# One of three bit shifts of VectorE's exponentials done by accumulating DMAs, with a ring of four PSUM banks, exponentials of two tiles and 133 packs on VectorE

## The chip, the core and the metric

The kernel runs on one core of a Trainium2 chip. The core has TensorE (PE, matmuls; its weight loads are shown as PEld), VectorE (DVE), ScalarE (ACT), GpSimd (POOL) and SyncE (SP), each with a queue of its own that it works through in order, and 16 DMA engines that all queues share. On-chip memory is SBUF (128 partitions) and PSUM (8 banks of 128 x 512 fp32, where matmuls write). The metric is device microseconds of one execution; the median of some runs is compared.

## The reference

Two attention blocks over the same x (2048 tokens, 512 features, 32 heads of 16) are mixed by a gate. Block A is softmax attention over all 2048 x 2048 pairs of each head, which is nearly all of the work. Block B is linear attention with softmax features.

```python
g = sigmoid((x * gate_w).sum(-1, keepdims=True))
# A: scores = q @ k.T * 16**-0.5 ; p = softmax(scores) ; o = p @ v ; a = o @ A_wo
# B: phi = [softmax(q @ w_phi), softmax(-(q @ w_phi))], the same for k
#    kv = phi_k.T @ v ; z = phi_k.sum ; b = (phi_q @ kv / (phi_q @ z + 1e-6)) @ B_wo
out = g * a + (1 - g) * b
```

## The kernel before

**Block A by packs.** A unit is one head's scores of 128 keys against 512 queries, one PSUM bank. Four units (four heads, whose 16 features sit in four 32-row strips of TensorE, so their score matmuls run side by side) make a pack; 16 packs (`kt`, the key tiles) make a group, and 32 groups (four query chunks of eight) make the 512 packs. A pack's probabilities, 128 keys x 512 queries for each head, are multiplied with V by four matmuls in four 32-column strips, which add up over a group's 16 packs in one PSUM bank. V carries a column of ones, so the same matmuls give the softmax denominator.

**Two ways to an exponential.** Most packs go over ACT: `_qk` (matmuls of L963) writes scores into a ring of `RING = 5` banks, `_exp` (L1011) turns three and two tiles in turn into bf16 in the buffer ET, `_pv` (L1077) multiplies with V. The score matmuls of one exponential wait for the exponential two before it, which read the same banks; in PE's queue they come first when they can run. The other packs, listed by `AWAY` (five bits for each group, for the tiles `KT0 + KTS * n`, here 1, 4, 7, 10, 13), go over VectorE: 121 packs. `_vector_bits` (L903) computes one tile as `uint16(score * a + b)`, whose bits, read as bf16, are a piecewise linear exponential. To smooth it, the sum of four such numbers is used, whose bits are shifted by 0, 30, 62 and 95; the last two are multiplied with a copy `vc` of V scaled by 0.75. `_vector_terms` (L919) makes the three shifted copies in the buffer `vp` from the buffer `va`, for two packs (4096 elements a partition) or one (2048) at a time, and `_pv_terms` multiplies each of the four with V on PE, again L1077. So a VectorE pack costs DVE four tiles of L903 and three shares of L919, and PE sixteen matmuls where an ACT pack needs four. `va` holds two pairs of packs.

**Banks.** The banks outside the ring are shared: one holds the group's sum, one or more are lent to each projection, VectorE score tile or output in turn (`acquire`, `release`).

**The order of the work** is set in Python before anything runs. Each instruction is an `Op` with engine, assumed cost, dependencies and a priority `prio` counted in packs; `Plan.order` puts the ops of each engine into a fixed order by these costs, and `SHIFT` moves the priorities of some hundred ops by hand-given amounts. `LAT`, `TURN`, `lat=` are assumed latencies. `emit` writes the queues with semaphore waits. So a wait on the chip that is longer than was assumed is not reordered: the queue stands. `_fill` (L1084) and the loop in `_qk` (L984) put filler matmuls where PE would have little to do.

**Around it.** `_proj_*` compute K, Q, V and evict them with DVE (L656, L664, L675, L697, L720); Q goes on by DMA from SP (L677). `_norm` divides a group's sum by its denominators on DVE and sends it by DMA (L1148) and a transposing DMA (L1363) to the output projection (L1457); the last group is normalized by `_norm_last` in two halves without DMA (L1107 to L1117). `_gate` computes the gate for the four query chunks by four matmul groups on TensorE (L736) and four transposes (L741). Block B's softmaxes run on DVE and ACT between (L1252 to L1309; the ACT part is L1281).

Of the kernel before, what the change touches and what calls it, by code (L numbers as in the profile page):

```python
# [22 lines left out]
SHIFTS = ((30, 0), (62, 1), (95, 1))  # L23
# [20 lines left out]
class Op:  # L44
    def __init__(self, eng, fn, cost, name, prio, rel, kind, lat):
        self.eng, self.fn, self.cost, self.name = eng, fn, cost, name
        self.prio, self.rel, self.kind, self.lat = prio, rel, kind, lat
        self.deps = []
        self.users = []
        self.left = 0  # L50
        self.need = False
        self.acquire = None
        self.release = None
        self.sem = None
        self.start = self.end = None
        self.commit = None
        self.array = 0.0
        self.filler = 0
        self.slack = None
        self.fits = True  # L60
        self.pad = False
        self.tiles = []
        self.filled = 0
        self.tag = None

# [38 lines left out]
class Plan:  # L104
# [190 lines left out]
    def emit(self, nc, ctx):  # L295
# [6 lines left out]
        count = dict.fromkeys(self.ENGS, 0)  # L302
        for e, q in self.queues.items():
            for o in q:
                if o.name.startswith("dma"):
# [71 lines left out]
class _Kernel:  # L377
    RING = 5
# [4 lines left out]
    NB, LEAD = 4, 16.0  # L383
    FIRST = 5
    KT0, KTS, NKT = 1, 3, 5
    KEEP = 13
    GAP, KDUE, VDUE, GATE = 3.45, -16.25, -11.75, 14.0
    TURN = 1.5
    LAST, RAMP, PART = 8.0, 48, 24
    STEP, BITS, TERM, PVX, NORM, QDUE, PUT = 0.625, -80, 5.5, 0.8, 2, -22.0, 3.8  # L390
# [29 lines left out]
    def _memory(self, ctx):  # L420
# [54 lines left out]
        self.va = sb("va", [P, 2, 2, self.NB, QCH], U16)  # L475
        self.warm = self.bq[:, 0, 0:QCH]
        self.wpp = self.bq[:, 3, 0:4 * P].rearrange("p (c j) -> p c j", c=4)
        self.gwb = self.bq[:, 0, QCH:2 * QCH].rearrange("p (c m) -> p c m", c=4)
# [59 lines left out]
    def _consts(self):  # L538
# [21 lines left out]
        self.b_zero, self.b_warm, self.b_gwb = B(), B(), B()  # L560
        op("DVE", lambda e: e.memset(self.warm, 1.0), 0.3, writes=[self.b_warm], prio=-95)
# [24 lines left out]
    def _projections(self):  # L586
# [13 lines left out]
        for j in range(NQC):  # L600
            if j == 0:
# [3 lines left out]
                self._proj_k0(1, 4)  # L605
# [61 lines left out]
    def _proj_q(self, qc, cp):  # L667
# [12 lines left out]
                 prio=due, lat=1.6)  # L680
# [44 lines left out]
    def _gate(self):  # L725
        op, NQC = self.plan.op, self.NQC
        b_gwb, last = self.b_gwb, []
        op("POOL", lambda e: e.tensor_copy(self.gwb, self.gw[:, :, None].to_broadcast([P, 4, P])), 1.0,
           reads=[self.b_gw], writes=[b_gwb], name="gwb", prio=15)
        z = self.onTA[:].rearrange("p s r j -> p (s r j)").bitcast(F32).rearrange("p (q b d) -> p q b d", q=NQC, d=32)  # L730
        for qc in range(NQC):
            job = Job()

            def mm(e, qc=qc, job=job):
                for c in range(4):
                    ins = e.matmul(self._bank(job), self.gwb[:, c, :], self.xT[:, c, QCH * qc:QCH * qc + QCH],  # L736
                                   start=(c == 0), stop=(c == 3))
                return ins
            m = op("PE", mm, 4 * self.c_pe(512), reads=[self.b_xT[qc], b_gwb], name="gate", prio=self.GATE + qc, rel=self.GATE - 6,
                   acquire=job)  # L740
            last.append(op("DVE", lambda e, qc=qc, job=job: e.transpose(  # L741
                z[:, qc].rearrange("p b d -> p (b d)"), self._bank(job)), 0.74, deps=[m], name="gate_t", prio=self.GATE + qc,
                release=job))
        flat = self.gh[:].rearrange("p r q b -> p (r q b)")
        col = z[:, :, :, 0].rearrange("p q b -> p (q b)")
        for r, sign in ((0, -1.0), (1, 1.0)):
            last.append(op("DVE", lambda e, r=r, sign=sign: e.tensor_scalar(
                self.gh[:, r].rearrange("p q b -> p (q b)"), col, sign, None, op0=ALU.mult), 0.2,
                deps=last, name="gate_z", prio=22))
        for b in self.b_onTA[0] + self.b_onTA[1]:  # L750
            b.readers = last[-2:]
        a = op("ACT", lambda e: e.activation(flat, flat, ACT.Exp), 0.2, deps=last, name="gate_exp", prio=24)
        self.b_g = Buf()
        op("DVE", lambda e: e.tensor_scalar(flat, flat, 1.0, None, op0=ALU.add), 0.25, deps=[a], writes=[self.b_g],
           name="gate_h", prio=24)
# [9 lines left out]
    AWAY = (15, 3, 9, 7, 27, 30, 29, 28, 26, 14, 15, 31, 14, 15, 27, 15, 15, 31, 23, 22, 31, 27, 13, 30, 27, 23, 11, 29, 31, 31, 21, 31)  # L765

    SHIFT = (
        ("p12", 11.5), ("k5", 3.5), ("k4", -8.5), ("v1", -2.5), ("p30", 10.5), ("p6", 13), ("p13", 1), ("p22", 7),
        ("p15", -5), ("q1", 3), ("w0", -13.5), ("p18", 6), ("b1", -9.5), ("v2", -4.5), ("x1", 2), ("v4", 6), ("p21",
        8), ("p2", 1), ("k1", -3), ("p26", -1.5), ("k6", 2), ("b4", -2.5), ("p9", -2), ("p0", 4.5), ("b42", 0.5),  # L770
        ("x4", -7.5), ("b20", -4), ("b55", 2.5), ("p40", 4), ("b52", -6.5), ("g1", 10), ("p36", 2), ("p38", 7),
        ("x33", -0.5), ("p31", 8), ("d0", -3.5), ("p34", -0.5), ("p32", -6.5), ("p39", 1), ("v9", 7), ("b68", -8.5),
        ("b65", -10.5), ("e2", -3.5), ("p62", -8), ("p54", -2), ("p47", -4), ("p59", -0.5), ("x77", 6), ("b87", 4),
        ("x65", 5.5), ("t84", -7.5), ("t65", 0.5), ("p75", -3), ("p70", 0.5), ("x68", -6), ("p72", 4.5), ("b93",
        6.5), ("x55", 11), ("b77", 5.5), ("b90", 7.5), ("a0", -1.5), ("p89", 1), ("p79", -0.5), ("g4", 9), ("x90",
        10), ("b97", 11.5), ("p92", 5), ("p94", 6.5), ("p104", 10.5), ("e5", -1.5), ("g5", 1.5), ("x103", -3),
        ("t90", 12), ("p98", -7.5), ("e4", -6), ("g6", 12), ("q5", 1.5), ("p124", -6), ("x138", -4), ("x122", 5),
        ("p140", -1.5), ("p126", -10.5), ("g7", 2), ("p127", -10), ("p121", 6.5), ("x141", -12), ("p116", -0.5),
        ("p137", -13.5), ("t125", -9), ("p113", -2), ("b132", -2.5), ("b125", -8.5), ("b138", -8), ("a4", -9),
        ("p136", -12), ("x109", 11), ("b154", 8.5), ("e8", 6), ("p112", 5.5), ("g8", 1), ("p152", 11), ("e11",  # L780
        -10.5), ("p157", -3), ("p149", -13.5), ("p158", -8), ("t154", -5), ("b170", 6), ("p155", 8.5), ("t148", 1),
        ("e9", 6), ("p147", -0.5), ("p144", 2.5), ("b167", 3), ("p171", 2.5), ("p172", 10), ("p159", 8), ("p168",
        8.5), ("p163", -7.5), ("p162", 0.5), ("a8", 9), ("x177", 11.5), ("p192", -11.5), ("p194", 2.5), ("p188",
        -2), ("g11", 1.5), ("e13", -1.5), ("p190", -8), ("x199", 10.5), ("p181", 8), ("b199", -4.5), ("p184", 11.5),
        ("p195", -2.5), ("b196", -5.5), ("d12", -13.5), ("p219", 4), ("x209", -13), ("p207", -8), ("p210", -8),
        ("p204", -8.5), ("t209", 11), ("p203", 3), ("p232", 12.5), ("p233", 8), ("f0", -5.5), ("b241", 8.5),
        ("x234", 3.5), ("t225", 12), ("a12", 14), ("p254", 3.5), ("p240", -14), ("b260", -1), ("p245", -11.5),
        ("p242", -13), ("b234", -12.5), ("p236", -8), ("b263", -11), ("g14", 2), ("p251", 12.5), ("b257", 8), ("h0",
        -8), ("t257", -11), ("t241", 2), ("b279", -3), ("x260", 13.5), ("p256", 3.5), ("p255", 8), ("p268", 6),
        ("p246", -0.5), ("p264", 2), ("p270", -3.5), ("p258", -1.5), ("p274", 5), ("p284", 2), ("g16", -11.5),  # L790
        ("x257", 6), ("b301", -8.5), ("p277", 9.5), ("p286", 3), ("p275", -11.5), ("p272", -2), ("t279", 10),
        ("b289", 7.5), ("b285", -0.5), ("p287", 14), ("p291", -5.5), ("b311", 3), ("p307", 2.5), ("p296", 1.5),
        ("p303", 2), ("p294", -4), ("b324", -10.5), ("p315", 8), ("p306", -12), ("t289", -5.5), ("x311", 8),
        ("p300", 10.5), ("p302", 14), ("x289", -4), ("o0", -8), ("p304", 8), ("x292", 8), ("p297", 5), ("p293", 2),
        ("b327", -6), ("h5", -10.5), ("n5", -9), ("x317", -3), ("o3", 3), ("p318", -4), ("n4", -9), ("p332", -4),
        ("p323", 2), ("p331", 4.5), ("q11", 0.5), ("b333", 13.5), ("p338", -9.5), ("p341", -1), ("x349", 14),
        ("h10", -7), ("p380", -10), ("p371", 6.5), ("p363", 6.5), ("p376", 12.5), ("o4", -8), ("o5", -3), ("p377",
        -1), ("b372", -13.5), ("h8", -4.5), ("x372", 8.5), ("o6", -11.5), ("h9", 10.5), ("p367", -0.5), ("p374",
        -1), ("p373", 2), ("x359", -9), ("g21", -1.5), ("p366", -6), ("x381", -4), ("b381", 1.5), ("x362", -2.5),
        ("p386", -1), ("p396", 0.5), ("b397", 5.5), ("n9", -4.5), ("b417", 13.5), ("f3", -8), ("b413", 2), ("b404",  # L800
        6), ("p414", -1.5), ("x385", 0.5), ("p411", -2), ("p409", 1.5), ("p392", 3.5), ("p400", 8), ("p416", -5.5),
# [717 lines left out]
```

## Time and profile before

| | |
|---|---|
| median of 3 runs | 759.11 us (758.89 to 759.82) |
| the profiled execution | 759.64 us, its span 757.8 us |
| granted TensorE clock | 0.999 |
| ACT busy | 740.4 us, of it L1011 712.2 |
| DVE busy | 730.0 us, of it L903 314.4 and L919 221.6 |
| PE busy | 718.0 us |
| POOL busy | 8.1 us, all in the first 60 us |
| DMA | 21.68 MB, at most 78 GB/s in a slice after the first two |

The span runs from the first to the last instruction; the execution's own time is a little longer. Busy time is the union of an engine's records: two instructions of one engine can overlap in the records, so the mean length of one is longer than the step from one to the next. The idle time "before" a group says what the engine waited for; a wait of an engine that is not the bound costs nothing. In the chain of work in order of time, each piece is either work or an engine's queue, and its length is what it adds to the end.

### The profile page before, as it was taken

To read this page: it belongs to the slowest core of one execution; us is meant where nothing else is said; L and a number is where in the kernel's file an instruction comes from. 1 tells how busy PE (TensorE), PEld (TensorE's weight loads), DVE (VectorE), ACT (ScalarE), POOL (GpSimd) and SP (SyncE) were. 2 spreads that over 40 slices of the span, in tenths; PEclk is the share of its full clock that TensorE was granted. 3 is DMA by queue.
4 is the path that set the end of the run, shared out by engine and by line. 5 is a ranking of instruction groups with operands and counts; after the bars stand their busy time and mean duration, and the time that the engine had idled before them with its cause. 6 is when DMAs were issued, how large, how long until landed. Compare 5 with 4: busy or idle time off the path is not lost.

```text
span 757.8 us, 16775 instructions
## 1 busy us (share of the span) xinstructions
PE 718.0 (95%) x7172; PEld 229.8 (30%) x7241; DVE 730.0 (96%) x1138; ACT 740.4 (98%) x646; POOL 8.1 (1%) x17
## 2 busy tenths in 40 slices
PE   8999999999999999999999999999999998999997
PEld 3334333342322232232222222223232222222222
DVE  6989899999999999999999999999999999999997
ACT  6999999999999999999999999999999999999995
POOL 3000000000000000000000000000000000000000
PEclk9999999999999999999999999999999999999999
DMA  9300100000010010000003101411103102301120
GB/s 212 130 2 1 15 8 10 14 7 16 2 16 8 8 16 8 6 11 7 18 9 63 23 12 25 71 29 23 29 29 65 21 16 35 78 13 25 12 26 29
DMA packets 88745, 21.68 MB, mean 29 GB/s; under 512 B 81632, under 2 KB 88160, under 8 KB 88672
## 3 DMA queue, kind: packets, MB, share of 16 engines
q1 hardware_dynamic: 86944, 20.10, 13.8%
q8 instruction: 56, 0.92, 0.5%
q10 hardware_dynamic: 1728, 0.52, 0.3%
q14 instruction: 17, 0.14, 0.1%
HBM read 4.21 MB, written 2.10 MB: 8 GB/s over the span
## 4 chain that ended last, share of the span: by engine, by line
ACT 64%; DVE 21%; PE 12%; DMA 1%; issue 1%; SPq 1%; DVEq 0%
ACT ET L1011 62%; DVE va L903 9%; DVE vp L919 6%; PE ps L963 5%; PE ps L1077 3%; ACT bq L1281 3%; PE ps L641 2%; DVE btree L1270 1%; DVE bq L1279 1%; PE ps L714 1%; DVE T L1129 1%; SPq L677 1%; DMA xT<-in_A_x_dram 1%; PE ps L984 1%; DVE V L720 1%
## 5 line engine op out<-in xcount | busy, mean ns | idle before, releaser
L1011 ACT ACTIVATE ET<-ps 128x1536 bf16<-128x1536 f32 x626 | 712.2, 1345 | 7.1 <-PE ps L963 6.2
L963 PE MATMUL ps<-qT,kT 32*128 32x512 bf16 x2048 | 312.1, 384 | 17.7 <-ACT ET L1011 8.5
L903 DVE TENSOR_SCALAR va<-ps 128x512 uint16<-128x512 f32 x484 | 314.4, 681 | 6.3 <-PE ps L963 4.9
L919 DVE TENSOR_SCALAR vp<-va 128x4096 uint16<-128x4096 uint16 (+1 forms) x204 | 221.6, 1097 | 0.2
L963 PEld LDWEIGHTS ps<-qT,kT 32*128 32x128 bf16 x2048 | 80.8, 91 | 263.0 <-ACT ET L1011 157.2
L1077 PE MATMUL ps<-ET,V 128*32 128x512 bf16 x1564 | 149.0, 386 | 0.3
L1077 PE MATMUL ps<-vp,vc 128*32 128x512 bf16 x968 | 84.5, 384 | 0.9 <-DVE vp L919 0.9
L1077 PEld LDWEIGHTS ps<-ET,V 128*32 128x32 bf16 x1564 | 39.3, 95 | 65.0 <-issue 51.0
L641 PE MATMUL ps<-WB,xT 128*128 128x512 bf16 x169 | 50.8, 383 | 4.4 <-issue 1.5
L1084 PE MATMUL ps<-kT,zero 128*32 128x512 bf16 x580 | 50.2, 385 | 0.0
L1077 PE MATMUL ps<-va,V 128*32 128x512 bf16 x484 | 47.8, 385 | 0.0
L1077 PE MATMUL ps<-vp,V 128*32 128x512 bf16 x484 | 46.2, 384 | 0.7 <-DVE vp L919 0.6
L641 PE MATMUL ps<-xT,WA 128*128 128x512 bf16 (+1 forms) x107 | 30.6, 373 | 3.6 <-issue 2.3
L1077 PEld LDWEIGHTS ps<-vp,vc 128*32 128x32 bf16 x968 | 21.9, 95 | 35.2 <-issue 18.0
L1281 ACT ACTIVATE bq<-bq 128x2048 bf16<-128x2048 bf16 x16 | 32.1, 2024 | 0.0
L1252 DVE CAST bq<-ps 128x512 bf16<-128x512 f32 x32 | 21.7, 683 | 2.9 <-PE ps L641 2.8
L1129 DVE STREAM_TRANSPOSE T<-ps 128x512 f32<-128x512 f32 x31 | 22.0, 709 | 0.6 <-PE ps L1077 0.3
L714 PE MATMUL ps<-WA,xT 128*128 128x128 bf16 x256 | 20.4, 220 | 0.5 <-DVE V L720 0.3
L1457 PE MATMUL ps<-WoA,onTA 128*128 128x512 bf16 x62 | 19.3, 382 | 1.0 <-DVE onTA L1117 0.9
L1279 DVE TENSOR_TENSOR bq<-bq,btree 128x2048 bf16<-128x2048 bf16 x16 | 19.4, 1214 | 0.0
L1084 PEld LDWEIGHTS ps<-kT,zero 128*32 128x32 bf16 x580 | 12.6, 94 | 22.1 <-issue 20.3
L641 PEld LDWEIGHTS ps<-WB,xT 128*128 128x128 bf16 x192 | 11.9, 97 | 23.9 <-issue 14.4
(87 smaller groups left out, 346.2 us busy)
## 6 DMA issues: line engine op xcount, KB each, us to landing
turned<-T SPq DMA_DIRECT2D x240, 8.0 KB, 1.8
qT<-qs SPq DMA_DIRECT2D x120, 16.0 KB, 1.8
WB<-in_B_wqkv_dram SPq DMA_DIRECT2D x1, 1536.0 KB, 7.4
out_dram<-WB SPq DMA_DIRECT2D x12, 128.0 KB, 1.9
WA<-in_A_wqkv_dram SPq DMA_DIRECT2D x3, 384.0 KB, 5.6
WoA<-in_A_wo_dram SPq DMA_DIRECT2D x1, 512.0 KB, 8.5
WoB<-in_B_wo_dram SPq DMA_DIRECT2D x1, 512.0 KB, 8.3
WA<-in_A_wqkv_dram ACTq DMA_DIRECT2D x3, 128.0 KB, 4.0
```

Of the source, the lines that this page charges most:

```text
L641: ins = e.matmul(self._bank(job)[:, 0:n], lhs(c), rhs(c), start=(c == 0), stop=(c == 3))
L714: ins = e.matmul(self._bank(job)[:, P * tt:P * tt + P], self.xT[:, c, QCH * j + TOK * tt:QCH * j + TOK * tt + TOK], self.WA[:, 2, c, P * c ...
L903: parts.append(op("DVE", lambda e, j=j, job=job: e.tensor_scalar(self.va[:, pair, side, j, :], self._bank(job), SCALE * LOG2E * 128.0, (12 ...
L919: self.plan.op("DVE", lambda e, k=k, shift=shift: e.tensor_scalar(flat(self.vp[:, k]), flat(self.va[:, pair]), float(shift), None, op0=ALU ...
L963: return e.matmul(out, self.kT[32 * i:32 * i + 32, cp, kt * TOK:(kt + 1) * TOK], self.qT[32 * i:32 * i + 32, s, :], start=True, stop=True, ...
L1011: o = plan.op("ACT", lambda e: e.activation(self.ET[:, a % NS:a % NS + n, :], self.ps[:, self._ring(a):self._ring(a) + n, :], ACT.Exp, sca ...
L1077: ins = e.matmul(self._bank(ot)[32 * i:32 * i + 32, :], V[:, v0:v0 + 32], tile(), start=(kt == 0), stop=(kt == self.NT - 1), tile_position ...
L1084: ins = e.matmul(self._bank(ot)[32 * i:32 * i + 32, :], self.zero[:], self.kT[:, 0, 0:QCH], start=False, stop=False, tile_position=(0, 32 ...
L1129: op("DVE", lambda e: e.transpose(T1[:, side].rearrange("p b s -> p (b s)"), src()), 0.635, deps=last, writes=[b_T1[side]], name="n_t1", p ...
L1252: [lambda e, b, k=k: e.tensor_copy(bq[:, k].rearrange("p (g s v) -> p g s v", g=8, s=2)[:, :, 0, :], b.rearrange("p (g v) -> p g v", g=8))],
L1279: run("b_sub", two(2048), lambda e, out=out, t=t: e.tensor_tensor(out, p, spread(t[:, :, 0], 32), ALU.subtract), at, [pos, tree[side]], [buf])
L1281: op("ACT", lambda e, side=side: e.activation(sides[side], sides[side], ACT.Exp, scale=1.0 - 2 * side), self.c_act(2048) + 0.04, reads=[bu ...
```

## The change

- **The shift by 30 goes.** `SHIFTS` keeps 62 and 95, so L919 makes two copies and `vp` shrinks by a third; `va` grows to three pairs (`NVA`).
- **It is added in place.** A pack's unshifted bits are multiplied with V first; then, when both other copies are made too, 30 is added to every element of `va`, and `va` is multiplied with V once more. For all packs but those of the last group the addition is a DMA that POOL issues, from a DRAM tensor `step` full of 30, with `accum_op=add`, 128 partitions x 4096 bytes; in the last group it is one VectorE instruction. The product after it stands `PVX = 4.0` packs after the pack's place (it was 0.8), the first `VALUES = 4.0` packs ahead. The plan assumes 3.1 us on POOL and 2.6 us to landing.
- **The ring has four banks**, exponentials are of two tiles always, and one bank more is shared.
- **133 packs** go over VectorE, at tiles 1, 3, 5, 7, 9 of a group.
- The gate is computed for all four chunks in one bank by column strips, with one transpose, and spread by 16 small DMAs of SP's; `_norm_last` goes, and the last group is normalized by `_norm` without DMAs; some assumed latencies and all of `SHIFT` are new.

By the program's instructions: exponentials of two tiles 312 to 758, of three 313 to 0; L903 484 to 532; L919 over two packs 159 to 118, over one 45 to 30; in-place shifts on VectorE 0 to 5, by DMA 0 to 128; matmuls 7243 to 7201; SP's DMAs gain 17. In the changed kernel L903, L919, L963, L1011, L1077 and L1084 stand on L942, L959, L1004, L1052, L1137 and L1144; the DMA is L1119.

```diff
-SHIFTS = ((30, 0), (62, 1), (95, 1))
+SHIFTS = ((62, 1), (95, 1))
+FIRST_SHIFT = 30
...
-    RING = 5
+    RING = 4
...
-    NB, LEAD = 4, 16.0
+    NB, LEAD, NVA = 4, 10.0, 3
+    VALUES, IN_PLACE, SLACK = 4.0, (496, 497, 498, ...), 6.0
...
-    KT0, KTS, NKT = 1, 3, 5
-    KEEP = 13
+    KT0, KTS, NKT = 1, 2, 5
+    KEEP = 11
...
-    TURN = 1.5
-    LAST, RAMP, PART = 8.0, 48, 24
-    STEP, BITS, TERM, PVX, NORM, QDUE, PUT = 0.625, -80, 5.5, 0.8, 2, -22.0, 3.8
+    TURN = 3.2
+    ADD, LANDING = 3.1, 2.6
+    LAST, RAMP, PART = 6.0, 48, 24
+    STEP, BITS, TERM, PVX, NORM, QDUE, PUT = 0.8, -80, 0.0, 4.0, 2, -22.0, 3.8
...
-        self.va = sb("va", [P, 2, 2, self.NB, QCH], U16)
+        self.va = sb("va", [P, self.NVA, 2, self.NB, QCH], U16)
+        self.step = nc.dram_tensor("step", [P, self.NB * QCH], U16, kind="Internal").ap()
...
+        row = self.va[:, 0, 0].rearrange("p n q -> p (n q)")
+        o = op("POOL", lambda e: e.memset(row, FIRST_SHIFT), 2.0, prio=-60)
+        self.o_step = self.dma("SP", "step", lambda e: e.dma_start(self.step, row), cost=0.6, deps=[o], prio=-8, lat=4.0)
...
-            b = min(a + (2 if len(self.exps) % 2 else 3), len(self.mine))
+            b = min(a + 2, len(self.mine))
...
+        first = values(lambda: va, ready, [b_va], max(group + 1, p - self.VALUES), f"i{p}")
+        if p in self.by_dma:
+            add = self.dma("POOL", f"add{p}", lambda e: e.dma_start(va.rearrange("p n q -> p (n q)"), self.step, accum_op=ALU.add),
+                           cost=self.ADD, deps=b_va.readers + [self.o_step], prio=p - self.VALUES + 1, lat=self.LANDING)
+            add.slot = 2 * pair + side
+            add.fn = [add.fn]
+        else:
+            flat = va.rearrange("p n q -> p (n q)")
+            add = self.plan.op("DVE", lambda e: e.tensor_scalar(flat, flat, float(FIRST_SHIFT), None, op0=ALU.add),
+                               0.07 + self.NB * QCH * 0.00026, deps=list(b_va.readers), name="v_step", prio=p - self.VALUES + 1)
+        add.tag = f"i{p}"
+        b_va.readers = [values(lambda: va, ready + [add], [], p + self.PVX, f"x{p}")]
         for tile, buf, scaled in self.terms.pop(p):
...
+            values(tile, ready + [self.o_vc[g8 // 2] if scaled else None], [buf], p + self.PVX, f"x{p}", V)
...
-        if g == self.NPACK // self.NT - 1:
-            return self._norm_last(qc, lambda: self._bank(self.ot[g]), last, self.onTA[:, qc % 2, g8 // 2, :], 16 * g + 17.0,
-                                   self.ot[g])
```

## The prediction

> **What bounds it now.** I read the page's busy times first, then the busy times by stretch, then the chain of work in order of time, and last the groups by shape. The page's head:
>
> ```profile
> span 757.8 us, 16775 instructions
> ...
> PE 718.0 (95%) x7172; PEld 229.8 (30%) x7241; DVE 730.0 (96%) x1138; ACT 740.4 (98%) x646; POOL 8.1 (1%) x17
> ```
>
> Two stretches of the second view (the columns are PE, PEld, DVE, ACT, POOL, then clock, DMA share, GB/s), in which the reader is to see two engines filled at once:
>
> ```profile
> 200.00:300.00 100.00, 95.39 (x937) 29.37 (x944) 99.50 (x154) 100.00 (x87) 0.00 (x0) 1.00 0.06 10
> ...
> 600.00:700.00 100.00, 94.91 (x955) 28.45 (x967) 97.66 (x156) 99.89 (x88) 0.00 (x0) 1.00 0.18 34
> ```
>
> ACT is never idle from 20 to 700 us but for 1.8 us by the stretches. Its idle 17 us lie at the start (first exponential at 8.48 us) and at the end (last one over at 748.6 us). DVE is 0.5 to 3% behind it, so the chain runs through both. The time falls only as far as ACT's work falls, provided that PE and DVE keep up.
>
> The chain gives what an instruction costs when the next stands right behind it (start, length, what; lengths in the group view hold some 0.2 us that the next one overlaps on ACT, 0.08 on DVE):
>
> ```profile
> 226.29 0.92 ACT ET L1011
> 227.21 1.79 ACT bq L1281
> 228.99 60.11 ACT ET L1011 x53
> ...
> 360.93 1.80 DVE va L903 x3
> ...
> 376.97 1.14 DVE vp L919
> ```
>
> An exponential of two tiles issues in 0.92 us. The 53, which alternate three and two tiles, take 60.11, and other such stretches give 2.267 a pair, so three tiles take 1.347: a tile 0.427, an instruction 0.066. A VectorE tile (L903) takes 0.60, a shift over two packs (L919) 1.13, over one pack 0.60.
>
> **ACT's work.** The groups by shape:
>
> ```profile
> L1011 ACT ACTIVATE ET<-ps 128x1536 bf16<-128x1536 f32 x313 | 487.2, 1556 | 7.1 <-PE ps L963 6.2
> L1011 ACT ACTIVATE ET<-ps 128x1024 bf16<-128x1024 f32 x312 | 354.3, 1135 | 0.0
> L903 DVE TENSOR_SCALAR va<-ps 128x512 uint16<-128x512 f32 x484 | 314.4, 681 | 6.3 <-PE ps L963 4.9
> ...
> L919 DVE TENSOR_SCALAR vp<-va 128x4096 uint16<-128x4096 uint16 x159 | 191.5, 1214 | 0.2
> ```
>
> 133 packs instead of 121 go to VectorE, so ACT has 1516 tiles instead of 1564: 48 x 0.427 = 20.5 us less. They come in 758 instructions instead of 626: 132 x 0.066 = 8.7 us more. **Net -11.8 us.** The sixteen L1281 instructions stay; the gate's exponential shrinks by about 0.1.
>
> **DVE's work.** 48 more tiles: +28.8. Shifts over two packs fall from 159 to 118 (-46.3), over one pack from 45 to 30 (-9.0); five in-place shifts in the last group are added (+3.0). The gate's four transposes become one and the last normalization is done whole: about -3. Sum -26.5, so DVE's busy time goes to about 703.5 us. This takes nothing off the end by itself, since ACT is the longer; it is what lets DVE take 12 more packs.
>
> **PE's work and the smaller ring.** The product of a pack's unshifted and 30-shifted bits was two sets of four matmuls, and still is. Over all, matmuls go from 7243 to 7201: 192 more on VectorE's packs, 48 fewer on ACT's, 152 fewer fillers L1084, 34 fewer L984. But score groups go from 626 to 758, and each change between row tiles, column tiles and whole-array matmuls costs. In the timeline a set of four column matmuls follows another by 0.215 us and one of another kind by 0.32 us, so a change is 0.105. Priced so along the program's order, PE's work is 696 us before and 702 after: 92% of the span before, 94% of the shorter one. With a ring of 5 the next scores had 0.92 or 1.35 us of exponential above them in turn; with 2 + 2 tiles it is always 0.92. Walking both orders with these prices (scores start when the exponential two before ends, and need 0.45 us), ACT waits 1.3 us in the old order, near the trace's 1.8, and 4.5 us in the new: **+3.2 us.** If a set costs 0.22 and a change 0.11 it is 3.0 and 7.4, so +4.4; if the DVE slack takes waits for shared banks away, it can be zero.
>
> **Start and end.** The new order puts all 16 V matmuls of the first 512 tokens (1.06 us in the trace) before the second half of Q0, and the V copy (0.60) before its copy on DVE; the scores now start at 8.05 us, held by DVE. I get the first exponential at about 9.2 instead of 8.48; the wait of 0.29 at 13.4 may go. **+0.6 us**, between 0 and +1. The 2048-wide memset on POOL (1.80 for the like of it) delays only a memset that pack 32 needs. At the end the last group was normalized in two halves:
>
> ```profile
> 749.79 0.45 DVE L1107 STREAM_TRANSPOSE T<-ps 128x256 f32<-128x256 f32 x1 [0.55 <-PE ps L1077]
> ...
> 753.24 0.45 DVE L1117 STREAM_TRANSPOSE onTA<-T 128x256 bf16<-128x256 bf16 x1
> ```
>
> From 749.79 to 753.69, then two stores' evictions. Whole, by the rows of the other groups: 0.71 + 0.16 + 0.25 + 0.42 + about 0.70 = 2.24 us, then four projections and two evictions on each of DVE and ACT, 1.3 us. The last eviction ends some 1 us earlier: **-1.0 us**, within 0 and -1.5.
>
> **The accumulating DMAs.** 128 packs get their 30 from a 512 KB transfer, issued by POOL, that reads a DRAM constant and adds it to the tile. The trace has no DMA of POOL's and no accumulation. The nearest rows of the DMA view (KB each, us to landing):
>
> ```profile
> WB<-in_B_wqkv_dram SPq DMA_DIRECT2D x1, 1536.0 KB, 7.4
> out_dram<-WB SPq DMA_DIRECT2D x12, 128.0 KB, 1.9
> ...
> WoA<-in_A_wo_dram SPq DMA_DIRECT2D x1, 512.0 KB, 8.5
> ```
>
> From below: 1.9 for the first 128 KB and 384 KB at WB's 207 KB/us, 3.8 us, plus an issue of 0.43 (WB's on SP): 4.2. If the target must also be read, twice the bytes: 1.9 + 4.3 and 0.4, 6.6. From above: WoA, which landed behind WB with the DMA engines 99% busy, 8.5, plus WoA's issue of 1.55: 10. I take 5.5, between the first two, since the DMA engines were at most a few tenths busy after 60 us. The Trainium skill ("DMA: Bandwidth & Descriptors", Anatomy of one DMA) gives about 2.0 us plus bytes over 436 KB/us for a transfer issued by GpSimd, an estimate of 3.2 us for this one; by it the cover below holds with room; the trace shows no such transfer.
>
> What covers it: an add waits for the first values (PE) and both remaining shifts (DVE). I counted in the order how many exponentials lie between its last release and PE's wait for it: 7 at least (8 of 128), 8 for 10, 9 for 22, 10 for 22, more for 66. At 0.92 us, less 1.2 for a shift still to run, the cover is 5.2, 6.2, 7.1, 8.0 us and up. So 5.5 costs 8 x 0.3 = 2 us at most, and the 0.4 us by which scores can be late under an exponential (0.92 less the 0.45 they need) absorb that: I take **0**. With 6.6 it is 15 us, with 10 some 200. Behind the waiting matmul stand the next scores, in order on PE, and ACT waits for those. Behind a late add on POOL stands only the next add; it never delays loads, which SP issues. Their landings may grow with 64 MB more traffic (at the first 20 us' 215 GB/s one takes 2.4 us, 128 take 312 of the span, so there is room); Q's and the normalization's transfers have tens of us.
>
> **Sum.** -11.8 + 3.2 + 0.6 - 1.0 + 0 = -9.0: span 748.8 us. The profiled execution took 759.64 for its 757.8, so 1.84 lies around it: 750.6. It lay 0.53 above the median of the three runs, 759.11, so 750.1; I say 750.0.
>
> **Rivals.**
> - *The adds land late.* If release to landing is above about 6.3 us, the waits on PE (10 us there, by the covers above) eat the 9 us gained; at 7 us they sum to 22, giving 772, at 8 us to 61, about 810, less what one wait spares the next. For: PE and POOL are in order, buffers of three pairs turn over every 30 us or so (74 pairs over the span). Against: the low rows. Chance 0.18.
> - *DVE's shifts and POOL's issuing exclude each other.* L919 handles 4096 elements in 1.13 us, 3.6 per ns, where L903 handles 512 in 0.60: it is another mode, and the trace, whose POOL is still after 60 us, cannot say what POOL may do beside it. If an add must let two shifts pass (2 x 1.13), 5.5 becomes 7.8, and the covers give 53 us of waits: about 800. If instead each add holds DVE for 0.5 us, DVE's 703.5 grows by 64 and becomes the bound: about 797; this decides from 0.14 us each, as DVE has some 17 us to spare beyond its idle time of today (748.8 less 703.5, less 27.8). Against: an add follows its own pair's shifts, so mostly L903 runs beside it. Chance 0.06. The Trainium skill ("SBUF — State Buffer", SBUF: two separate sides) speaks for this one: a VectorE operation in a mode that takes both ports keeps GpSimd from writing descriptors until it is over, 620 ns becoming 3100; nothing in the trace agrees or disagrees.
> - *PE becomes the bound here and there*: its 94% with waits for banks and places that my walk leaves out. Another 4 to 8 us: 754 to 758. Chance 0.11.
> - *ACT waits for nothing and the end gains its 1.5*: 745. Chance 0.04.
>
> The forecast, 745.5 to 753.5, has 0.61. Faster by over 0.2% (1.5 us, about what a measurement tells) is the forecast, the 745 and most of the PE case: 0.73; within it 0.04; slower 0.23. The range 745 to 766 leaves out the worse half of the slow cases.
>
> **What would show it.** ACT's L1052 at 758 x 0.92 = 697 us with idle time of 22 us or so; DVE near 704; PE's waits for ACT still the largest, and waits of PE for the adds near nothing; landing of the POOL transfers under 6 us; a VectorE shift still 1.13. I am wrong if PE waits for the adds by tens of us, if L959 lengthens, or if ACT idles in mid-span.

## The result, and the profile after

The changed kernel takes **842.3 us** (median of four runs, 835.75 to 877.66) against 759.24 before: **slower, ratio 1.101 [1.098, 1.104]**. The forecast was 750.0 (745 to 766). Single executions of this kernel differ by some per cent and each has its own granted clock (835.75 us at 0.944, 877.66 at 0.908), so the interval rests on the fastest ones, and the medians of the runs with full adds below are good to some per cent only. The profiled execution took 836.22 us for a span of 834.4. Its head, from the first three views of the page:

```profile
span 834.4 us, 17041 instructions
...
PE 761.7 (91%) x7199; PEld 225.4 (27%) x7199; DVE 709.9 (85%) x1127; ACT 736.1 (88%) x778; POOL 129.3 (16%) x146
...
PEclk9899999999899999999976989969899999979999
DMA  9364274535636586556696564985557968559671
...
q0 software_dynamic: 18432, 67.12, 47.5%
```

ACT and DVE have less to do, as forecast (740.4 and 730.0 before), but no engine is full any more. The clock row has its deep dips (7 and below) from the 21st slice (417 us) on, and the DMA row is no longer empty: q0, the queue of the adds, alone takes 47.5% of the 16 engines. The same stretches as before, and then two longer ones (columns as before):

```profile
200.00:300.00 100.00, 94.56 (x943) 27.12 (x935) 92.00 (x137) 94.59 (x102) 18.08 (x19) 0.97 0.61 105
...
600.00:700.00 100.00, 95.79 (x914) 27.10 (x916) 94.52 (x155) 95.94 (x103) 18.13 (x19) 0.98 0.79 129
```

```profile
100.00:400.00 300.00, 289.78 (x2832) 87.89 (x2832) 282.81 (x432) 291.40 (x307) 45.63 (x49) 0.99 0.56 94
400.00:800.00 400.00, 352.76 (x3242) 95.94 (x3240) 328.31 (x530) 337.62 (x356) 64.05 (x70) 0.90 0.75 117
```

ACT (the fourth engine) loses 8.6 us from 100 to 400 us, but 62 from 400 to 800, at a mean clock of 0.90. What PE waited for (us in total, times, longest one), from the view of waits:

```profile
PE ps L1414 <- DMA phiT<-bq: 22.6, 3, 11.4
PE ps L1137 <- DMA va<-step: 14.4, 18, 2.0
PE ps L1440 <- DMA WT<-nb: 6.9, 2, 4.1
PE ps L1004 <- DMA step<-va: 5.3, 1, 5.3
PE ps L1004 <- DMA qT<-qs: 3.6, 2, 3.0
```

All five are transfers. Only the second is the one that the prediction weighed. `phiT` and `WT` are transposing loads of block B's data (SP issues them from about 400 us on); before, `phiT` landed 3.2 us after issue (5.0 at most) and PE never waited for it. The groups and the DMA view:

```profile
L1052 ACT ACTIVATE ET<-ps 128x1024 bf16<-128x1024 f32 x758 | 706.8, 1082 | 88.2 <-PE ps L1004 82.2
L942 DVE TENSOR_SCALAR va<-ps 128x512 uint16<-128x512 f32 x532 | 340.0, 682 | 55.6 <-PE ps L1004 54.0
...
va<-step POOLq DMA_DIRECT2D x128, 512.0 KB, 7.0
...
phiT<-bq SPq DMA_TRANSPOSE x16, 5.0
WT<-nb SPq DMA_TRANSPOSE x16, 6.2
```

The last two rows in the kernel before:

```profile
phiT<-bq SPq DMA_TRANSPOSE x16, 3.2
WT<-nb SPq DMA_TRANSPOSE x16, 2.5
```

Of ACT's 88.2 us of idle time, 82.2 end on PE's scores. The chain of work in order of time shows the largest loss:

```profile
413.35 1.21 DVE va L942 x2
414.56 0.05 SPq L1392
414.61 0.04 issue
414.65 1.34 SPq L1392
415.99 0.04 issue
416.03 3.37 SPq L1392
419.40 0.04 issue
419.44 20.41 DMA phiT<-bq
439.85 0.09 issue
439.94 0.38 PE ps L1414 x4
440.33 0.54 PE ps L1004 x2
```

One transposing load took 20.41 us. The matmul that needs it stands in PE's queue ahead of the next scores, so all engines stop. What follows is in ACT's timeline (start, length, in brackets the idle time before and its cause) and the windows:

```profile
440.91 1.02 ACT L1052 ACTIVATE ET<-ps 128x1024 bf16<-128x1024 f32 x1 [11.56 <-PE ps L1004]
442.42 1.02 ACT L1052 ACTIVATE ET<-ps 128x1024 bf16<-128x1024 f32 x1 [0.49 <-PE ps L1004]
```

```profile
430.00:436.00 6.00, 0.00 (x0) 0.00 (x0) 0.00 (x0) 0.00 (x0) 0.86 (x1) 0.50 1.28 57
...
446.00:454.00 8.00, 8.00 (x61) 1.50 (x60) 4.85 (x9) 5.38 (x6) 0.86 (x1) 0.52 0.37 57
454.00:465.00 11.00, 11.00 (x122) 3.42 (x114) 10.95 (x19) 11.00 (x13) 2.61 (x3) 1.00 0.75 113
```

While PE stands still, its granted clock goes to 0.50 (the column before the DMA share), and it stays there until about 454 us, 14 us after the restart. In that time the exponentials come 1.5 us apart instead of 0.92, each after a wait for PE's scores. From 430 to 436 the DMA engines are more than full (1.28; two queues' packets overlap in the records) and move only 57 GB/s.

### The profile page after: what moved, and what is told of

Read it like the earlier page. It is cut to its first block, busy times and chain, and to the rows that moved or that the text cites. A ratio compares the mean times of both kernels' runs of the same rounds, so it can differ in the third digit from the quotient of the medians.

```text
span 834.4 us, 17041 instructions
## 1 busy us (share of the span) xinstructions
PE 761.7 (91%) x7199; PEld 225.4 (27%) x7199; DVE 709.9 (85%) x1127; ACT 736.1 (88%) x778; POOL 129.3 (16%) x146
## 3 DMA queue, kind: packets, MB, share of 16 engines
q0 software_dynamic: 18432, 67.12, 47.5%
## 4 chain that ended last, share of the span: by engine, by line
PE 33%; DMA 24%; DVE 24%; SPq 9%; ACT 8%; issue 2%; POOL 0%; DVEq 0%
PE ps L1004 13%; DMA va<-step 12%; DVE va L942 11%; PE ps L1137 10%; ACT ET L1052 7%; DMA phiT<-bq 6%; DVE vp L959 5%; PE ps L655 4%; DMA WT<-nb 3%; SPq L1177 3%; SPq L1392 2%; SPq L691 2%; PE ps L1440 1%; PE ps L1486 1%; SPq L770 1%
## 5 line engine op out<-in xcount | busy, mean ns | idle before, releaser
L1052 ACT ACTIVATE ET<-ps 128x1024 bf16<-128x1024 f32 x758 | 706.8, 1082 | 88.2 <-PE ps L1004 82.2
L942 DVE TENSOR_SCALAR va<-ps 128x512 uint16<-128x512 f32 x532 | 340.0, 682 | 55.6 <-PE ps L1004 54.0
L1004 PE MATMUL ps<-qT,kT 32*128 32x512 bf16 x2048 | 339.6, 398 | 17.6 <-DMA step<-va 5.3
L1119 POOL DMA_DIRECT2D va<-step x128 | 119.8, 1051 | 665.7 <-DVE vp L959 400.3
L959 DVE TENSOR_SCALAR vp<-va 128x4096 uint16<-128x4096 uint16 (+1 forms) x148 | 161.7, 1107 | 16.1 <-PE ps L1137 15.8
L1004 PEld LDWEIGHTS ps<-qT,kT 32*128 32x128 bf16 x2048 | 83.6, 91 | 303.1 <-ACT ET L1052 207.8
L1137 PE MATMUL ps<-ET,V 128*32 128x512 bf16 x1516 | 150.5, 398 | 2.1 <-DVE nb L1422 1.6
L1137 PE MATMUL ps<-va,V 128*32 128x512 bf16 x1064 | 101.5, 398 | 14.7 <-DMA va<-step 14.4
L1137 PE MATMUL ps<-vp,vc 128*32 128x512 bf16 x1064 | 99.4, 402 | 2.1 <-DVE vp L959 2.0
L1137 PEld LDWEIGHTS ps<-ET,V 128*32 128x32 bf16 x1516 | 38.6, 96 | 63.2 <-issue 51.9
L1137 PEld LDWEIGHTS ps<-va,V 128*32 128x32 bf16 x1064 | 25.4, 95 | 61.4 <-issue 30.8
L1144 PE MATMUL ps<-kT,zero 128*32 128x512 bf16 x428 | 39.6, 396 | 0.0
L1137 PEld LDWEIGHTS ps<-vp,vc 128*32 128x32 bf16 x1064 | 24.6, 96 | 38.3 <-issue 25.6
L1414 PE MATMUL ps<-kvbd,phiT 128*128 128x68 bf16 x128 | 9.6, 205 | 22.7 <-DMA phiT<-bq 22.6
L1440 PE MATMUL ps<-WoB,WT 128*128 128x512 bf16 x64 | 21.7, 424 | 7.4 <-DMA WT<-nb 6.9
```

Of the source, the lines that this page charges most:

```text
L942: parts.append(op("DVE", lambda e, j=j, job=job: e.tensor_scalar(self.va[:, pair, side, j, :], self._bank(job), SCALE * LOG2E * 128.0, (12 ...
L959: self.plan.op("DVE", lambda e, k=k, shift=shift: e.tensor_scalar(flat(self.vp[:, k]), flat(self.va[:, pair]), float(shift), None, op0=ALU ...
L1004: return e.matmul(out, self.kT[32 * i:32 * i + 32, cp, kt * TOK:(kt + 1) * TOK], self.qT[32 * i:32 * i + 32, s, :], start=True, stop=True, ...
L1052: o = plan.op("ACT", lambda e: e.activation(self.ET[:, a % NS:a % NS + n, :], self.ps[:, self._ring(a):self._ring(a) + n, :], ACT.Exp, sca ...
L1119: add = self.dma("POOL", f"add{p}", lambda e: e.dma_start(va.rearrange("p n q -> p (n q)"), self.step, accum_op=ALU.add), cost=self.ADD, d ...
L1137: ins = e.matmul(self._bank(ot)[32 * i:32 * i + 32, :], V[:, v0:v0 + 32], tile(), start=(kt == 0), stop=(kt == self.NT - 1), tile_position ...
```

## The experiments

All times are medians beside a run of the kernel before (759.2 to 759.9). "Step apart" means that the constant 30 is stored to DRAM from a corner of `vp` that is idle then, instead of from `va`'s first tile:

```diff
-        row = self.va[:, 0, 0].rearrange("p n q -> p (n q)")
+        row = self.vp[:, 1, 1].rearrange("p n q -> p (n q)")
...
-        self.b_va[0][0].readers = [self.o_step]
+        self.b_vp[1].readers = [self.o_step]
```

**1. Is it the adds at all?** Tiny adds keep every instruction, queue and wait, and move almost nothing:

```diff
-e.dma_start(va.rearrange("p n q -> p (n q)"), self.step, accum_op=ALU.add)
+e.dma_start(va.rearrange("p n q -> p (n q)")[:, 0:8], self.step[:, 0:8], accum_op=ALU.add)
```

Tiny adds alone:

> Each of the 128 accumulating DMAs adds only 8 of the 2048 elements of each partition (16 bytes instead of 4096); every queue's order, every wait and every semaphore is that of the changed kernel. So the shift by 30 is left out for nearly all elements. Theory (the bulk of the adds costs the time, by their own landing, by what they do to the transposing DMAs, and by the half TensorE clock after each standstill): the adds land in 2 to 3 us, the phiT transposes in 3 to 5 us, the granted clock is 0.99 or more, and the time is the 750 forecast plus some 6 us for the wait on the store of the constant, 753 to 760. Rival 1 (the ring of four and the two-tile exponentials leave TensorE too little cover): ACT still waits tens of us for scores, 810 to 840. Rival 2 (POOL's issuing and VectorE's shifts exclude each other): issuing stays at 0.87 us and so does the loss, over 800.

760.0 us, ratio 1.0004 [0.9995, 1.0014]: 82 of the 83 us are gone. PE's longest wait is now 6.7 us for the store of the constant. With that moved as well:

> Adds of 8 elements instead of 2048 (the shift by 30 is left out for the rest), and the constant stored from a corner of vp, so that nothing early waits for that store. Theory (without the adds' bulk and the start's wait all other steps of the forecast hold): ACT saturated from about 10 us to the end, 746 to 752. Rival (the 12 us that the kernel with tiny adds lost before 100 us have another cause than that wait, such as the order of the start): 757 to 762.

750.9 us, ratio 0.988 [0.987, 0.990]: 0.9 us above the forecast's 750.0, though without the two things that went wrong. Its page and 400 to 500 us, in which ACT is full and the clock whole:

```profile
span 750.2 us, 16972 instructions
...
PE 719.8 (96%) x7130; PEld 225.1 (30%) x7199; DVE 705.5 (94%) x1127; ACT 728.0 (97%) x778; POOL 129.8 (17%) x146
```

```profile
400.00:500.00 100.00, 98.01 (x967) 28.73 (x974) 97.43 (x159) 100.00 (x108) 19.40 (x22) 1.00 0.27 39
```

The same POOL work is there (129.8 us). So the loss isn't the issuing, nor VectorE and POOL shutting each other out, since both are as before: the bytes of the adds are the cause.

**2. Traffic or accumulation?** Plain copies of the same size (`accum_op` left out, so the last products are those of a constant 30):

> The same 128 DMAs of POOL's, of the same 512 KB from the same DRAM tensor to the same place and in the same order, but plain copies without accumulation (the products after them are then those of the constant 30). Theory, if the reading and writing back of the target is what makes a 4 KB packet slow (344 ns in the changed kernel): packets of about half that, landing at 4 to 5 us instead of 7.0, PE's waits for them near nothing, 760 to 785. Rival (64 MB of traffic beside the transposes is enough, accumulated or not): landing 6 to 7 us, phiT transposes still up to 20 us, 815 to 840.

777.5 us, ratio 1.024 [1.020, 1.029].

```profile
q0 software_dynamic: 18432, 67.12, 25.9%
...
va<-step POOLq DMA_DIRECT2D x128, 512.0 KB, 4.4
```

Landing is 4.4 us, and q0's share falls from 47.5 to 25.9% of the span: a packet of 4 KB (18432 of them) takes 0.259 x 774.1 x 16 / 18432 = 174 ns, with accumulation 0.475 x 834.4 x 16 / 18432 = 344. So plain traffic costs 17.5 us over tiny adds (760.0, with the same wait for the store), and accumulating it another 65.

**3. The constant's store alone.**

> The changed kernel, but the constant 30 is stored to DRAM from a corner of vp that is written late, so that the first tiles on va do not wait for that store. Theory (the wait of 5.5 us at 26 us, with 20 to 60 us at a clock of 0.91 behind it, is lost time of its own): 6 to 10 us less, 826 to 831. Rival (the time lost there is only shifted to the next wait for a DMA): within 2 us of the changed kernel's 836.

Missed: 842.7 us (814 to 860), no gain that can be told in this scatter, although the same edit gives 9.1 us with tiny adds. It is the reference of the next runs with adds, which all have the step apart.

**4. Where in the span?** phiT and WT are loaded only in the second half. The adds are full on one side of pack 256 and tiny on the other (the tiny side lacks its 30):

```diff
+            full = slice(0, self.NB * QCH) if p < 256 else slice(0, 8)
```

> The adds have their full size for the packs below 256 and 8 of 2048 elements a partition behind them, so the bits of the later packs lack their 30; the order of all queues and the place of the constant are those of the run with all adds tiny (750.9 us). The transposing loads of block B (phiT, WT) lie behind 385 us, in the other half. Theory T (most of the loss comes from transposes and other small transfers that land late behind the adds, and from the slow clock after the stops that they cause): 755 to 765. Rival D (most of the loss comes from PE's own waits for the adds, which are spread over the whole span): about half of the 92 us that lie between full and tiny adds, so 785 to 800.

> The reverse: tiny adds for the packs below 256, full ones behind them; the bits of the earlier packs lack their 30. Theory T: 800 to 840, nearly all of the loss, with PE waiting for phiT and WT by 20 us or more. Rival D: 785 to 800 here too.

760.9 us (61 full adds, +10.0 over all tiny) and **840.2** (67 full adds, +89.3). PE's waits in the late run, and the DMA view of its 396 to 416 us:

```profile
PE ps L1415 <- DMA phiT<-bq: 38.8, 3, 26.4
PE ps L1138 <- DMA va<-step: 8.8, 11, 2.7
PE ps L1415 <- issue: 7.8, 1, 7.8
```

```profile
q1 hardware_dynamic: 3085, 0.77, 66.8%
q0 software_dynamic: 334, 1.22, 48.8%
...
va<-step POOLq DMA_DIRECT2D x4, 512.0 KB, 23.9
phiT<-bq SPq DMA_TRANSPOSE x4, 20.1
```

Four adds and four transposing loads: with tiny adds such loads land in 3.3 us (median of the run), and the median of all adds of the changed kernel is 7.0. Here the loads need 20 and the adds 24. An add's packet takes 0.488 x 20 x 16 / 334 = 468 ns there, against 0.530 x 100 x 16 / 2592 = 327 at 200 to 300 us of the changed kernel, where q1 is at 7%. Both sides lose. An add in flight isn't enough for that: in the changed kernel each of the 16 phiT loads has at least one beside it, and nine of them still land within 5.3 us; the other seven take 7.0 to 20.4.

**5. The place of the add, or the half of the span?** In the late run 22 of the 67 full adds are made tiny: those beside the phiT loads, or 22 others (some of which stand beside the WT loads).

```diff
-... if p >= 256 else slice(0, 8)
+... if p >= 256 and p not in (257, 259, 309, 311, 313, 321, ...) else slice(0, 8)
```

> As the run with full adds for the packs from 256 on (840.2 us), but 22 of its 67 full adds are made tiny: those issued from some 10 us before the transposing loads phiT to their end. Theory N (adds in flight beside the transposing loads make the loss: PE waits 46.6 us for phiT, and restarts at a low clock): 770 to 795, phiT landing below 5 us. Rival M (each full add costs alike, wherever it stands): 22/67 of the 89 us go, so 811, here and in the control.

> The control: 22 other adds of the 67 are made tiny, away from the phiT loads (some of them stand beside the WT loads); those beside phiT stay full. Theory N: 815 to 840, PE waiting for phiT by 30 us or more. Rival M: 811, as in the other.

**788.3** (778.2 to 792.0) and **825.7** us (802.1 to 830.6): by the medians 22 adds are worth 51.9 us beside phiT and 14.5 elsewhere. The two ranges don't overlap, and the first lies wholly below the 811 of the rival by which all adds cost alike, so the place matters; how much is rough, since the lowest times of the two lie 24 us apart and the medians 37. With the first, phiT lands at its old speed and is gone from PE's waits:

```profile
phiT<-bq SPq DMA_TRANSPOSE x16, 3.2
WT<-nb SPq DMA_TRANSPOSE x16, 5.5
```

In the second PE still waits 36.8 us for phiT. What the first leaves, 37 us over all tiny, still has collisions of the other kind (WT 5.5 instead of 2.5 us; PE waits 6.4 us for it and VectorE 12.0); I didn't take those apart.

**6. Does the size of the cost go with the bytes?** Adds of 1024 of 2048 elements (the other half of a tile lacks its 30):

> Every add covers 1024 of the 2048 elements a partition, 256 KB instead of 512; the other half of a tile lacks its 30. Packets are of 2 KB. If the loss is a threshold (a transfer costs nothing while it lands under the cover of 5 us, and the DMA engines have time between adds for the transposes): landing 4.5 to 5, time 753 to 770. If the loss goes with the bytes that the adds move: half of 92 us, about 797. If it goes with the count of packets, whatever their size: as with full adds, above 810.

764.6 us (761.1 to 767.7): half the bytes cost 13.7 of the 92 us. Landing 4.7 us, phiT 3.5, a packet of 2 KB 0.280 x 759.3 x 16 / 18432 = 185 ns. So the cost grows much faster than the bytes. Accumulating 256 KB keeps the DMA engines about as long as copying 512 KB plainly (q0 at 28.0 and 25.9% of the span), and costs about as much (13.7 and 17.5 us): what counts seems to be the time on the DMA engines, be it bytes or accumulation. A threshold, where the adds land under the shortest cover (5.2 us in the prediction) and leave the DMA engines gaps, fits the numbers, but no run moves the cover alone.

**7. Does the clock fall by itself?** All adds tiny, three exponentials repeated, each repeat behind the end of the one before:

```diff
...
+            for _ in range({150: 4, 250: 8, 350: 12}.get(k, 0)):
+                self.again += 1
+                once().then_inc(plan.again, 1)
+                e.wait_ge(plan.again, self.again)
+            return once()
```

> All adds tiny, as in the run of 750.9 us, but the exponentials 150, 250 and 350 are repeated 4, 8 and 12 times on ScalarE (same input, same output), which stops the scores for about 3.7, 7.4 and 11 us, 22 in all, with no transfer in play. Theory A (TensorE's granted clock falls by itself after a stop of about 10 us, and it takes some 13 us to come back): 775 to 785, the granted clock near 0.5 behind the longest stop, and exponentials 1.5 us apart there instead of 0.92. Rival B (the half clock seen beside the transfers has to do with the transfers): 771 to 774, granted clock 1.0 behind every stop.

787.5 us, above the range of theory A and far from B. PE stood still for 4.1, 8.4 and 12.6 us. ACT behind the longest stop:

```profile
388.49 1.02 ACT L1055 ACTIVATE ET<-ps 128x1024 bf16<-128x1024 f32 x1 [0.48 <-PE ps L1005]
389.99 1.02 ACT L1055 ACTIVATE ET<-ps 128x1024 bf16<-128x1024 f32 x1 [0.48 <-PE ps L1005]
391.50 1.02 ACT L1055 ACTIVATE ET<-ps 128x1024 bf16<-128x1024 f32 x1 [0.48 <-PE ps L1005]
```

```profile
376.00:383.00 7.00, 1.24 (x15) 0.81 (x16) 0.00 (x0) 6.84 (x8) 0.00 (x0) 0.50 0.00 0
...
394.00:399.00 5.00, 5.00 (x28) 0.87 (x25) 3.84 (x6) 3.11 (x4) 0.00 (x0) 0.50 0.10 10
399.00:404.00 5.00, 5.00 (x61) 1.23 (x58) 4.49 (x7) 4.53 (x5) 1.76 (x2) 0.95 0.16 27
```

The rhythm is that of the changed kernel, without a full add in play, and ACT waits for PE each time. The half clock lasts from the restart at 381.8 to about 399.5 us; behind the stop of 8.4 us it lasted some 5, behind that of 4.1 us some 4. The span is 35.2 us longer than with tiny adds alone; the 24 repeats take 1.03 each, 24.7, so 10.5 are after-effects. That the clock falls with a stop, without the transfers, is shown; what sets the length of its return is not.

**8. Other ways around.** The ring of four, with tiles two by two, on the kernel before (121 packs, three shifts):

> The kernel before with a ring of four banks, exponentials of two tiles always and one more shared bank, 121 packs on VectorE with all three shifts, no DMA adds. Theory (the ring costs only the fixed part of more instructions): 782 exponentials instead of 626, 156 x 0.066 = 10 us more on ACT, plus 2 to 4 us of waits for scores: 768 to 774. Rival 1 (the cover under a two-tile exponential is too short): ACT waits tens of us more, over 790.

Missed: 789.9 us, ratio 1.040 [1.038, 1.042]. ACT works 13 us more, where 10 were counted, and idles 34 us instead of 17. The likely reason is that the hand-made order belongs to the old ring, but no run shows it. Run e5, whose order was made for the new ring, comes out near the forecast sum; it doesn't show the ring alone. All 30s added by VectorE:

> The shift by 30 is added in place by VectorE for all 133 packs, no DMA adds, the constant's store stays. VectorE gets 128 x 0.60 = 77 us more, 782 us of work, and becomes the bound. Theory (VectorE's queue then sets the time): 795 to 820, so the DMA adds as they are in the changed kernel (836) cost more than the work that they take from VectorE. Rival (VectorE's idle time of today is enough to take much of it): under 785.

812.0 us, ratio 1.069 [1.064, 1.074], DVE busy 777.0: by the medians the transfers cost more than the VectorE work that they replace (842.7 with the step apart, though the lowest of its four times, 814.2, is level with this). And the order made anew with longer assumed times, first for the adds (`ADD, LANDING = 0.9, 6.6`), then for phiT (`lat=9.0`) and the other transposing loads too (`TURN = 7.0`):

> The changed kernel with full adds and the constant stored apart, and the plan's assumed times for an add set to what the trace shows: 0.9 us on POOL and 6.6 to landing instead of 3.1 and 2.6, 7.5 in sum instead of 5.7. Theory A (PE's direct waits for adds, 41 us in 55 waits, are most of the loss, and the order can cover them): those waits fall under 15 us and the time to 785 to 805. Theory B (what the adds do to the transposing DMAs, with landings up to 20 us, is most of it): the waits for phiT and WT stay, 810 to 835.

> As the run with the add's assumed times at 0.9 and 6.6, and besides the transposing DMAs assumed to land in 9.0 us (phiT) and 7.0 (WT, onTA) instead of 2.2 and 3.2. Theory A: no more than 8 us better than that run. Theory B: waits of PE for phiT and WT fall from 37 us to under 10 and the time is 15 to 35 us below that run, 770 to 795.

898.8 and 934.3 us: both missed, far above every time that was expected. PE's waits for adds grew to 29.1 and 46.9 us. A likely reason is that the last products moved while `SHIFT` and the three pairs of `va` stayed, but no run shows it. One thing did come as expected: in the second run PE no longer waits for phiT or WT, though phiT still lands after up to 19.6 us, so an order can cover them; what this order loses elsewhere is far more. No run points to a version with the whole addition that beats the kernel before: even with half of the bytes it is 0.7% slower.

## Why the prediction was wrong, point by point

- **ACT's work, net -11.8: right.** L1052 was forecast at 697 us and is busy 698.8 in e5. From the first exponential to the end of the last there are 740.2 us before and 732.2 in e5, -8.0; with PE's +3.2 the forecast was -8.6.
- **DVE at 703.5: right** (705.5 in e5; 709.9 in the changed kernel).
- **PE and the smaller ring, +3.2: right in kind, a little small.** In that stretch of e5 ACT idles 6.6 us where it idled 2.2 before, +4.4. The rival that PE becomes the bound is out there: ACT is full (100.00 of 100 us from 400 to 500).
- **Start, +0.6 within 0 to 1: wrong by size.** The first exponential comes at 9.88 us in e5, +1.4. And the step missed a wait: the constant is stored from `va`'s first tile, so VectorE's first score tile stands until the store has landed (8.9 us after issue), and PE behind it. With tiny adds that costs 760.0 - 750.9 = 9.1 us. It could be read in the diff: `b_va[0][0].readers = [self.o_step]`.
- **End, -1.0: right** (9.2 us after the last exponential before, 8.1 in e5).
- **The adds, "I take 5.5" and "I take 0": wrong, the step that failed.** The term of the sum for the adds was nothing, and there the 92 us between e5 and the run with full adds belong. Landing is 7.0 us in the median (5.3 to 19.6), close to the 6.6 that the text had priced for "if the target must also be read", and had passed over for a lower value because the DMA engines seemed idle: they were, before the adds filled them. The Trainium skill ("DMA: Bandwidth & Descriptors", Anatomy of one DMA), from which the prediction had worked out 3.2 us, has no accumulation in its formula: the plain copy took 4.4, the accumulating one 7.0, and the measurement decides.
- **"Their landings may grow ... so there is room": wrong, and the larger part.** The average was near enough (47.5% of the engines' span, against 312 us or 42% forecast). But adds come in twos and threes, an add holds all 16 engines for 144 packets x 344 ns / 16 = 3.1 us, and the transposing loads need them just then. The step says that a late add "never delays loads, which SP issues": it looked at the queues alone, and left out that both queues use the same 16 engines. phiT and WT, for which PE then waited 22.6 and 6.9 us, stood in no step. phiT landed after up to 20.4 us instead of at most 5.0. Experiments 4 and 5 put most of the loss there: 89.3 us in the half with these loads, 10.0 in the other.
- **The rival "the adds land late"** came, with its 772 at a landing of 7 us. As far as it goes it may have been well priced: the first half, where hardly anything else is hit, lost 10.0 us, so twice that would be 771. But it was only a part of the loss, and 0.18 was too little for the whole.
- **DVE and POOL shutting each other out: it happens, but costs nothing.** L959 over two packs takes 1214 ns as before, so VectorE isn't held. The issue of an add takes 0.86 us in the median, but most that meet such a shift stand until the shift is over. The twelve issues of the changed kernel that took longer than 1.24 us (2.19 at most) all have one beside them; ten end 0.08 to 0.13 us behind the end of a shift, and two stand behind one of the ten. One of them, and its shift:

```profile
314.85 1.56 POOL L1119 DMA_DIRECT2D va<-step  x1 [2.32 <-DVE vp L959]
```

```profile
315.07 1.22 DVE L959 TENSOR_SCALAR vp<-va 128x4096 uint16<-128x4096 uint16 x1
```

  That is the kind of wait of the Trainium skill's rule ("SBUF — State Buffer", SBUF: two separate sides), by which a DMA that GpSimd issues grows from 620 to 3100 ns beside a VectorE copy, as its descriptors wait for the end of the copy; 2.19 us is the most seen here. Run e5 has such issues too (2.18 at most) and reaches 750.9, so the rival's price of some 800 us is out.
- **Not foreseen at all: the clock.** Each of the stops that were looked at is followed by some microseconds at half clock, so a late transfer costs more than its lateness.

The ledger by runs: 759.2 before; 750.9 without the adds' bytes and the store's wait; 760.0 with that wait; 777.5 with it and plain copies; 842.3 with it and accumulation. That e5 comes so near the forecast is in part luck. The span of its profiled execution is 750.2 us, 1.4 above the forecast span: the start and the ring cost 2.0 more than forecast, and ACT's work (737.9 to 725.6 in that stretch) fell by 0.5 more. The median run then lies 1.1 below the profiled one. What stays open is why adds and transposing loads slow each other so much, beyond that both are on the same 16 engines; the runs show that they do, not how.

## What to carry to other kernels

Before work is moved to DMA, list every transfer that already stands near it and has little room, with its landing time and what queues behind it; an average share of the engines says nothing about that. The packets of an accumulating DMA took twice as long as plain ones here; price it so, and by its landing among its like, not alone. In a kernel whose order is fixed beforehand, a stop of 10 us costs more than 10 us, since TensorE restarts slowly.

## What the runs showed of the hardware

- Packets of 4 KB took 344 ns accumulating and 174 ns plain; accumulating ones of 2 KB, 185 ns. Such a transfer landed after 7.0 us (512 KB, accumulating), 4.4 (512 KB, plain) and 4.7 (256 KB, accumulating).
- A transposing load beside accumulating adds landed after up to 20.4 us in the changed kernel and 37.5 in the late run, against at most 5.2 with tiny adds; its issue on SP took up to 16.9 us instead of at most 1.6.
- The issue of an add on POOL that meets a VectorE shift (L959) took up to 2.19 us instead of 0.86 and, in ten of the twelve longest, ended 0.08 to 0.13 us behind the shift.
- After a stop of 12.6 us TensorE's granted clock was 0.50 for about 18 us, after one of 8.4 us for about 5, after one of 4.1 us for about 4. The Trainium skill ("TensorE: Matmul & The Clock Gate", Part 1: The HAM clock gate) has the full clock back after a busy window of about 3.4 us; the two shorter stops come near that, the longest does not, though PE shows as busy throughout (5.00 of 5 us in the row above).
